# A retention layer and an ELU feed-forward layer on one core: moving weight stores, chunk loads and three VectorE steps to other places of a hand-written order

## The chip, the cores and the metric

The kernel runs on one core of a Trainium2 chip. The metric is the device time of one execution in microseconds (us). A version is timed by the median of several executions; beside them one execution is recorded by the hardware profiler, and all durations below come from that one.

## The reference

Two layers one behind the other, all in float32. The first is a retention layer over B = 4 sequences, H = 8 heads, S = 768 tokens and D = 64 values for each head; the second is a feed-forward layer with ELU on the 4 x 768 = 3072 tokens of 8 x 64 = 512 values.

```python
gamma = 1.0 - 2.0 ** (-5.0 - np.arange(H)); scale = 1.0 / np.sqrt(D)
for t in range(S):
    state = gamma * state + outer(k[t], v[t])      # 64 x 64 for each sequence and head
    y[t] = scale * q[t] @ state
x = y.transpose(0, 2, 1, 3).reshape(3072, 512)
h = x @ w_in                                       # 512 x 2048
g = np.where(h > 0, h, np.exp(np.minimum(h, 0)) - 1)
return g @ w_out                                   # 2048 x 512
```

## The kernel before

**The tiles.** The 3072 tokens are six tiles of 512. A tile is four chunks of 128 tokens; the q, k and v of a chunk are one DMA of 1 MB (`load`, L102, issued at L113) into one of four buffers (`ldpool`), and then one multiplication of v by decay factors on POOL (`scale_v`, L287, operation at L293). Tiles 0 and 1 go through the layers by themselves. Tiles 2 and 3 are the first large block, tiles 4 and 5 the second (`for nb in range(NB)`); the "first large block" of the change is nb = 0.

**Retention** of a tile is cut into five steps (`retention_step`, L1544). Step 0 is the scores of q and k (`scores`, L324: two calls, one for each pair of chunks, in bursts of small matmuls listed as sc L319), step 1 the states (`states`, L373: two calls, matmuls listed as kv L359, then four sums on VectorE for each call; scores and states share four PSUM buffers, two for each call), and steps 2, 3 and 4 are the outputs (matmuls listed as y L415 and y L430), after each of which VectorE makes four products. Steps 2, 3 and 4 write the tile's x, which the first layer reads. The steps are put between the matrix products of another tile, where the order says so. Below, "visit 3" and "visit 4" are steps 3 and 4 of tile 2, which are called from the loop at L1622.

**The feed-forward layer by Strassen's method.** Each product of two matrices is cut into 2 x 2 blocks and made of seven block products; inputs of some of them are differences of blocks (made by VectorE), and their results are added up afterwards. In the second layer this is done twice, one inside the other: seven outer products, each of seven inner products. The inner product i of the outer product k is written (k,i) here. The stages that matter, with their times in the profile:

- 172 to 242 us: the second layer of tile 1 (`second_twice`, L903, matmuls at L924), outer order 1, 2, 6, 7, 5, 3, 4 (`ORDER2`), inner order 1, 2, 6, 7, 5, 3, 4 (`inner`). It is a generator which the loop at L1622 drives; each time it hands back a place ("first", "middle" or the end of an outer product), the loop looks into two dictionaries: VISITS (which visit of tile 2's retention comes here) and LOADS (which of chunks 12 to 15, that is tile 3, is loaded and scaled here). The number counts the outer products from 0, so (1, "first") is the first place inside the second one. `next_input` makes the inputs of later outer products on VectorE meanwhile, and `add` (L936) sums results of inner products.
- 242 to 303 us: the first layer of the first large block. `big_twice` (L1139, matmuls at L1152) makes four of the seven outer products of the first layer, each in two halves: eight halves, at = 0 to 7. A half holds the inner products in the order 1, 2, 6, 7, 5, 4, 3 (matmuls into the PSUM banks pa, pb and pd), and ScalarE copies some of their results (`lift`, L1163). Between them stand retention steps of tile 3, the inputs of the products to come (`xparts`, L1678), and stores of weights (below).
- 303 to 343 us: the other three outer products of the first layer, called M6, M4 and M5 by their numbers (`rest(m, 6)`, `rest(m, 4)`, `rest(m, 5)`; matmuls in `big_rest`, L1199), for eight slices m = 0 to 7 of the hidden values, in the loop over n at L1760. They are added into PSUM on top of a sum that ScalarE copied there (`seed`, L1650; `second_seed`, L1654, copies at L1656). `big_sum` (L1206, operation at L1208) makes the slices of the blocks C21, C12 and C22, `big_elu` (L1210) takes ELU of them (ScalarE at L1214 and L1215, VectorE at L1216), and `big_c11` (L1218, operation at L1220) completes the block C11.
- 343 to 446 us: the second layer of the first large block (`second_big`, L1233, matmuls at L1248, ScalarE's copies of results `ms` at L1256). The inputs of an outer product are four differences, called quarter inputs (`quarters_of`, L892, operations listed at L894); `next(sec)` makes one step of this generator, and its first four steps are the four quarter inputs of the first outer product.
- 446 to 536 us and 538 to 626 us: the same for the second large block, nb = 1.

**What sets the order.** Each engine runs its instructions in the order in which the program issues them; this order is written out by hand. All DMAs go through SP's queue, in program order, and SP holds at a DMA until its buffer is free; what is behind it in the queue is held too.

**Weights.** The combined weights of the second layers lie in DRAM (scratch), and pieces of 256 KB come into a ring of eight buffers `wq` (three more for tile 1). When a product is done with a piece, `done` (L833) hands the buffer back, and `fetch` (L826) issues the next weight DMA at once (L830). For the second large block the weights of its first layer are fetched in the same way, so the first block stores them in DRAM: `send_quarters(j)` (L867: quarters of the outer products j = 1, 2, 3, 7, six DMAs of 128 KB each) and `send_layer(j)` (L880: the planes of M4, M5 and M6, four DMAs of 256 KB each). They only fill a list, and `send_small` (L664) issues what is in it. Before the change a list names one store for each half (`stores`, L1695): none, quarters 2, quarters 3, plane 4, quarters 1, plane 6, quarters 7, plane 5.

**The three VectorE steps.** The last step of `xparts` is M4's input, `sub(t4_, b21, t2)` at L1120: one operation on 128 x 1024 values. In the order before, it comes behind `big_c11(0, 1)` of half 7 (L1732), an add of the same size, and behind `rest(0, 6)` and the second seed (L1755). In the loop over n, the last slice is n = 7 (LAST). At n = 6 two quarter inputs are made, at n = 7 two more ahead of `rest(7, 5)`, and then the sums of tile (slice) 7 into C12 and C22, which ScalarE waits for to take ELU of them. The loads of tile 4's chunks 16 to 19 (`bring`, L1669: load and scaling) stand in halves 4 and 5 and at n = 1 and n = 5.

## Time and the profile before

| what | value |
|---|---|
| median of three runs | 623.34 us (622.74, 623.34, 626.59) |
| the profiled execution: its own time | 628.01 us |
| its span from first to last instruction | 626.2 us |
| mean granted TensorE clock in it | 0.997 |
| instructions | 13424 |
| ScalarE's wait at L1163 for TensorE, over 32 copies | 46.3 us |
| POOL's wait at L293 for chunks, over 16 scalings | 159.8 us |
| bytes moved by DMA, mean rate | 125.14 MB, 200 GB/s |
| weight pieces of 256 KB: DMAs, median from issue to landing | 191, 3.1 us |
| chunks of 1 MB: DMAs, median from issue to landing | 22, 7.7 us |
| stores of 128 KB from `w_all`, and of 256 KB | 24 and 12; 4.1 and 5.2 us |

How to read it: the profile comes from one execution, which took 628.01 us; the span is the stretch in which instructions run. A line of the trace's groups has the engine, the name of the tile written, the line of the kernel, and behind an arrow what the engine waited for. PE is TensorE, DVE VectorE, ACT ScalarE, POOL GpSimd and SP the engine that issues the DMAs. In the list of waits of TensorE the three numbers are the summed wait, how many instructions had it, and the longest one. In a timeline a line has the start, the length and the instruction, and in brackets how long the engine stood idle before it and what ended that. Busy times of TensorE are modelled, so a busy share of 98% does not mean that nothing is left inside a matmul.

### The profile page before, as it was taken

To read this page: it belongs to the slowest core of one execution; us is meant where nothing else is said; L and a number is where in the kernel's file an instruction comes from. 1 tells how busy PE (TensorE), PEld (TensorE's weight loads), DVE (VectorE), ACT (ScalarE), POOL (GpSimd) and SP (SyncE) were. 2 spreads that over 40 slices of the span, in tenths; PEclk is the share of its full clock that TensorE was granted. 3 is DMA by queue.
4 is the path that set the end of the run, shared out by engine and by line. 5 is a ranking of instruction groups with operands and counts; after the bars stand their busy time and mean duration, and the time that the engine had idled before them with its cause. 6 is when DMAs were issued, how large, how long until landed. Compare 5 with 4: busy or idle time off the path is not lost.

```text
span 626.2 us, 13424 instructions
## 1 busy us (share of the span) xinstructions
PE 612.4 (98%) x5446; PEld 481.7 (77%) x5446; DVE 495.3 (79%) x776; ACT 260.9 (42%) x446; POOL 24.9 (4%) x30
## 2 busy tenths in 40 slices
PE   7899999999999999999999999999999999999998
PEld 5774568888888998888444888888888644688886
DVE  5759889989788875777788987898546788888885
ACT  5889744205542111236797310100144789511110
POOL 1012000000000010000110000120000000000000
PEclk8999999999999999999999999999999999999999
DMA  8798568889574997289941445773554422356552
GB/s 298 276 349 324 168 202 267 240 239 273 205 235 124 333 364 268 61 256 277 301 133 68 115 132 156 265 273 108 205 165 144 142 69 86 115 152 185 153 155 113
DMA packets 79278, 125.14 MB, mean 200 GB/s; under 512 B 6128, under 2 KB 46832, under 8 KB 74480
## 3 DMA queue, kind: packets, MB, share of 16 engines
q1 hardware_dynamic: 79216, 124.28, 61.1%
q8 instruction: 43, 0.70, 0.4%
q14 instruction: 19, 0.16, 0.1%
HBM read 94.63 MB, written 29.62 MB: 198 GB/s over the span
## 4 chain that ended last, share of the span: by engine, by line
PE 86%; DMA 6%; DVE 3%; SPq 1%; issue 1%; ACT 1%; DVEq 0%; ACTq 0%
PE pa L1248 15%; PE pa L1152 9%; PE pd L1248 7%; PE pa L1199 6%; PE pd L1152 4%; PE pd L1199 4%; DMA wq<-scratch_dram 4%; PE pb L1248 4%; PE pa L542 3%; PE x L632 3%; PE pa L765 3%; DMA chunk<-in_qkv_dram 2%; PE pb L1152 2%; PE pa L632 2%; PE pb L1199 2%; PE y L415 2%
## 5 line engine op out<-in xcount | busy, mean ns | idle before, releaser
L1256 ACT COPY ms<-pa 128x256 f32<-128x256 f32 x41 | 15.2, 370 | 104.0 <-PE pa L1248 101.0
L1248 PE MATMUL pa<-gC,wq 128*128 128x256 f32 x224 | 53.2, 382 | 0.3 <-ACT ms L1256 0.3
L1248 PEld LDWEIGHTS pa<-gC,wq 128*128 128x128 f32 x224 | 42.0, 190 | 7.5 <-issue 1.0
L1215 ACT ACTIVATE r<-r 128x512 f32<-128x512 f32 x64 | 40.3, 630 | 2.0
L1163 ACT COPY m<-pa 128x512 f32<-128x512 f32 x32 | 18.7, 585 | 46.4 <-PE pa L1152 46.3
L293 POOL TENSOR_TENSOR chunk<-chunk,vf 128x512 f32<-128x512 f32 x16 | 22.2, 1388 | 381.1 <-DMA chunk<-in_qkv_dram 159.8
L1260 DVE TENSOR_TENSOR res<-pd,ms 128x256 f32<-128x256 f32 x26 | 11.0, 422 | 24.2 <-PE pd L1248 14.1
L1152 PE MATMUL pa<-ts,wq 128*128 128x256 f32 x104 | 27.1, 385 | 0.7 <-ACT w_all L1163 0.7
L1248 PE MATMUL pa<-ts,wq 128*128 128x256 f32 x112 | 26.9, 383 | 0.3 <-ACT ms L1256 0.3
L1248 PE MATMUL pd<-w_all,wq 128*128 128x256 f32 x112 | 26.5, 379 | 0.0
L171 ACT ACTIVATE w_all<-wraw 128x1024 uint32<-128x1024 uint32 (+1 forms) x19 | 19.2, 1009 | 15.9 <-DMA wraw<-in_w_dram 5.2
L1248 PE MATMUL pd<-ts,wq 128*128 128x256 f32 x104 | 24.6, 379 | 0.0
L1230 DVE TENSOR_TENSOR gC<-w_all,gC 128x1024 f32<-128x1024 f32 x20 | 24.2, 1261 | 0.0
L1248 PEld LDWEIGHTS pa<-ts,wq 128*128 128x128 f32 x112 | 20.9, 190 | 3.7 <-ACT ms L1256 0.7
L1248 PEld LDWEIGHTS pd<-w_all,wq 128*128 128x128 f32 x112 | 21.3, 190 | 2.9
L1216 DVE SCALAR_TENSOR_TENSOR w_all<-r,w_all 128x512 f32<-128x512 f32 x32 | 21.9, 684 | 1.9 <-ACT r L1215 1.9
L1152 PEld LDWEIGHTS pa<-ts,wq 128*128 128x128 f32 x104 | 19.2, 190 | 5.5 <-ACT w_all L1163 1.1
L1248 PE MATMUL pa<-w_all,wq 128*128 128x256 f32 x96 | 22.9, 381 | 0.0
L173 ACT ACTIVATE w_all<-wraw 128x1024 fp8e4<-128x1024 f32 (+1 forms) x19 | 22.6, 1191 | 0.6
L1214 ACT ACTIVATE r<-w_all 128x512 f32<-128x512 f32 x32 | 20.0, 624 | 6.2 <-DVE w_all L1208 6.2
L1199 PE MATMUL pa<-gC,w_all 128*128 128x512 f32 x48 | 22.1, 592 | 0.0
L1199 PE MATMUL pa<-ts,wq 128*128 128x512 f32 x48 | 22.1, 592 | 0.0
(327 smaller groups left out, 1458.2 us busy)
## 6 DMA issues: line engine op xcount, KB each, us to landing
wq<-scratch_dram SPq DMA_DIRECT2D x191, 256.0 KB, 3.1
chunk<-in_qkv_dram SPq DMA_DIRECT2D x22, 1024.0 KB, 7.7
wraw<-in_w_dram SPq DMA_DIRECT2D x15, 1024.0 KB, 6.1
out_dram<-res SPq DMA_DIRECT2D x7, 512.0 KB, 2.9
scratch_dram<-gT SPq DMA_DIRECT2D x12, 256.0 KB, 4.3
wq<-scratch_dram SPq DMA_DIRECT2D x24, 128.0 KB, 3.0
scratch_dram<-w_all SPq DMA_DIRECT2D x24, 128.0 KB, 4.1
scratch_dram<-w_all SPq DMA_DIRECT2D x12, 256.0 KB, 5.2
```

Source lines behind the costliest of these rows:

```text
L171: nc.scalar.activation(flat, lo, AF.Copy, scale=2.0**-29)
L173: nc.scalar.activation(top, hi.bitcast(FP32), AF.Copy, scale=2.0**-120, saturate=False)
L293: eng.tensor_tensor(out=v, in0=v, in1=vf[:, i].unsqueeze(2).to_broadcast([C, H, D]), op=ALU.mult)
L542: nc.tensor.matmul(hp, lhsT=w[n][:, fi, j // 2, j % 2, :], rhs=xb[:, j, :], start=(j == 0), stop=(j == 3))
L632: nc.tensor.matmul(X[j][:, d, :], lhsT=w[j][:, d * P : d * P + P], rhs=x[j], start=(n == 0 and d == 0), stop=at_end, skip_group_check=True,)
L1152: nc.tensor.matmul(ps[:, f, :], lhsT=w[:, f, :], rhs=big_xs[j][k], start=(begin and f == 0), stop=True, skip_group_check=True,)
L1199: nc.tensor.matmul(ps, lhsT=w[:, k, :], rhs=layer_x[j][:, k], start=False, stop=(k == 1), skip_group_check=True,)
L1214: nc.scalar.activation(r, g, AF.Relu, scale=-1.0)
L1215: nc.scalar.activation(r, r, AF.Exp, scale=-1.0)
L1216: return lambda: nc.vector.scalar_tensor_tensor(g, r, -1.0, g, ALU.add, ALU.max)
L1230: nc.vector.tensor_tensor(out=quarter(to, r, t), in0=quarter(x, r, t), in1=quarter(y, r, t), op=op)
L1248: nc.tensor.matmul(ps, lhsT=w[:, f, :], rhs=ts[j][k][:, f // 2, f % 2, :], start=(begin and f == 0), stop=(f == 3), skip_group_check=True,)
```

## The change

No matrix product, no DMA and no operation of VectorE, ScalarE or POOL is added or taken away. What is moved:

- In tile 1's second layer, visit 3 goes from the end of the first outer product's place to (1, "first"), where visit 4 stood, and visit 4 to (1, "end"). The loads of chunks 14 and 15 go from (4, "middle") and (5, "first") to (5, "end") and (6, "middle"); those of 12 and 13 stay at their places, so that chunk 12's now stands ahead of visit 4 in the program.
- In the first half of the first large block, states(3, 0) stands in the middle, and scores(3, 1) and states(3, 1) at the end. Before, scores(3, 1) stood in the middle and both states at the end.
- The stores: planes 4 and 6 at half 0, quarters 2 and plane 5 at half 1, quarters 3 at half 2, quarters 1 at half 5 and quarters 7 at half 7. The number of DMAs and of bytes is the same.
- Chunks 16 to 19 are loaded and scaled at n = 0, 1, 3 and 5 of the loop over n, and no longer in halves 4 and 5.
- In both large blocks M4's input takes the place of `big_c11(0, 1)` at half 7, and that add goes behind `rest(0, 6)`, ahead of the second seed.
- In both large blocks the two quarter inputs at n = 6 go away from there: two of the four are made at n = 7 ahead of `rest(7, 5)`, and two behind the loop. So tile 7's sums into C12 and C22 stand ahead of the last two quarter inputs.

```diff
--- before.py
+++ after.py
@@ -1617,8 +1617,8 @@
         pass
     flush()
     retention_step(2, 2)
-    step, VISITS = 0, {(0, "end"): 3, (1, "first"): 4}
-    LOADS = {(1, "first"): 0, (2, "end"): 1, (4, "middle"): 2, (5, "first"): 3}
+    step, VISITS = 0, {(1, "first"): 3, (1, "end"): 4}
+    LOADS = {(1, "first"): 0, (2, "end"): 1, (5, "end"): 2, (6, "middle"): 3}
     for s in sec:
         if s == "first":
             step += 1
@@ -1692,11 +1692,11 @@
             if at in parts_of:
                 some(xparts, parts_of[at][place])
 
-        stores = [
-            lambda: None, lambda: send_quarters(2), lambda: send_quarters(3), lambda: send_layer(4, range(NQ)),
-            lambda: send_quarters(1), lambda: send_layer(6, range(NQ)), lambda: send_quarters(7),
-            lambda: send_layer(5, range(NQ)),
-        ]
+        stores = {
+            0: lambda: (send_layer(4, range(NQ)), send_layer(6, range(NQ))),
+            1: lambda: (send_quarters(2), send_layer(5, range(NQ))), 2: lambda: send_quarters(3),
+            5: lambda: send_quarters(1), 7: lambda: send_quarters(7),
+        }
         for at, (j, sub) in enumerate(ORDER1):
             if at == 4:
                 held_x = [ldpool.tile([P, 2048], FP32, name="chunk", tag="chunk") for _ in range(2)]
@@ -1720,7 +1720,7 @@
                 end("C11", 1)
             if nb == 0:
                 if at == 0:
-                    scores(3, 1)
+                    states(3, 0)
                 elif at == 1:
                     retention_step(3, 3)
             run(tail)
@@ -1728,31 +1728,32 @@
                 seed(0)
             next(cur)
             tail = cur
-            if at in (5, 7):
-                big_c11(0, at // 7)
+            if at == 5:
+                big_c11(0, 0)
+            if at == 7:
+                some(xparts, 1)
             if at == 6:
                 end("C11", 0)
             if at in (6, 7):
                 begin("C11", {6: 1, 7: 5}[at])
             if nb == 0:
                 if at == 0:
-                    retention_step(3, 1)
+                    scores(3, 1)
+                    states(3, 1)
                 elif at == 1:
                     retention_step(3, 4)
                     run(tail)
             side(at, 2)
-            if nb == 0:
-                if at in (4, 5):
-                    bring(groups[0], at - 4)
+            if nb == 0 and at in stores:
                 stores[at]()
                 send_small()
         sec = second_big(nb, (lambda: run(big_x(2))) if more else lambda: None)
         LAST = 2 * NQ - 1
         next(tail)
         rest(0, 6)
+        big_c11(0, 1)
         second_seed(0)
         end("C11", 4)
-        some(xparts, 1)
         run(tail)
         seed(1)
         begin("C11", 2)
@@ -1795,17 +1796,16 @@
                 end("C11", 3)
             if n in (0, 2):
                 begin("C11", 6 + n // 2)
-            if more and n in (1, 5):
-                bring(groups[0], 2 + n // 4)
+            if more and n in (0, 1, 3, 5):
+                bring(groups[0], (n + 1) // 2)
             if n == LAST:
                 next(sec)
                 next(sec)
             rest(n, 5)
             sum_("C12", n)
             sum_("C22", n)
-            if n == LAST - 1:
-                next(sec)
-                next(sec)
+        next(sec)
+        next(sec)
         next(sec)
         begin("C12", LAST)
         next(sec)
```

## The prediction

> **What bounds the kernel now.** I read the page's busy shares first, then its chain that ended last, then the waits of TensorE, then the timelines of TensorE, VectorE and SyncE around each wait. The shares and the chain:
>
> ```profile
> PE 612.4 (98%) x5446; PEld 481.7 (77%) x5446; DVE 495.3 (79%) x776; ACT 260.9 (42%) x446; POOL 24.9 (4%) x30
> ...
> PE 86%; DMA 6%; DVE 3%; SPq 1%; issue 1%; ACT 1%; DVEq 0%; ACTq 0%
> ```
>
> TensorE is busy for 612.4 of 626.2 us, and the change takes no matmul away. So an edit can gain only what TensorE waits. The list of TensorE's waits gives the places:
>
> ```profile
> PE pd L924 <- DMA wq<-scratch_dram: 1.3, 2, 0.9
> PE pd L1199 <- DVE ts L1120: 1.0, 1, 1.0
> PE pd L1199 <- ACT w_all L1163: 0.9, 1, 0.9
> ...
> PE y L430 <- issue: 0.8, 1, 0.8
> PE pa L1152 <- ACT w_all L1163: 0.7, 1, 0.7
> ...
> PE pa L1248 <- ACT ms L1256: 0.6, 2, 0.3
> ```
>
> These six lines (5.3 us) are all that the change can reach; the other waits lie before 172 us or where nothing moves. The chain in order of time shows that from 217 to 241 us the transfers set the pace:
>
> ```profile
> 217.40 8.62 DMA wq<-scratch_dram
> 226.04 7.42 DMA chunk<-in_qkv_dram
> 233.52 7.65 DMA wq<-scratch_dram
> ```
>
> **The change part by part.** (k,i) is inner product i of outer product k of tile 1's second layer; its 8 matmuls take 0.895 us (start to start in TensorE's timeline).
>
> *Visits 3 and 4 of tile 2 later.* No instruction is added. In the trace visit 3 runs from 195.24 to 197.95, with 0.83 us of "issue" in it, and visit 4 begins at 201.72. After the change (2,1), (2,2), (1,3), (1,4) begin at 195.24 and end at 198.8, visit 3 (2.71 - 0.83 = 1.88) ends at 200.7, (2,6), (2,7), (2,5) end at 203.4, and visit 4 follows. VectorE's four products of visit 4 (2.48 us at 202.48) move behind the fourth next_input step and the inputs of (6,.), which so come earlier; nothing reads tile 2's x before 236.42, so they cost nothing. The "issue" wait stands where 2 visits with one product between them follow each other. Visit 4, which has four products (3.6 us) ahead of it, shows none. After the change each visit has at least three ahead. Bounds 0 to -0.8; nearest row visit 4, so **-0.8**.
>
> The Trainium skill (Runtime: NRT & Kernel Launch, "Instruction fetch mechanics") says that instructions arrive in blocks of 256 while earlier ones run, and that crossing a block is mostly hidden. By that rule the burst of short instructions would not be what makes this wait, and spreading the bursts would gain 0 here and not 0.8. No row here shows which it is.
>
> *Load 12 stands ahead of visit 4 now.* It takes a buffer whose last reader is visit 4, so SP holds at it and the weight fetches behind it wait. In the trace it is issued 0.75 us after visit 4 begins (202.47), so now at 203.4 + 0.75 = 204.1, 1.7 later. The four fetches ahead of it go 2.7 earlier, since their products do; the three behind it (204.00 to 205.8) go at 204.5 to 205.2. So the transfers of this stretch change places and little time is lost. The next wait on weights, at 224.71 (0.2 now), has bounds -0.2 and +1.7; I take **+0.3**, near the lower end: the DMA share is only 0.67 in 202 to 204, so the time that SP holds is partly idle today.
>
> *Loads 14 and 15 later.* This is where a stall goes:
>
> ```profile
> 226.04 0.33 SPq L113 DMA_DIRECT2D chunk<-in_qkv_dram  x1
> ...
> 230.81 0.48 SPq L113 DMA_DIRECT2D chunk<-in_qkv_dram  x1
> ...
> 234.25 1.13 PE L924 MATMUL pd<-ts,wq 128*128 128x128 f32 x8 [0.34 <-DMA wq<-scratch_dram]
> ...
> 241.30 1.13 PE L924 MATMUL pd<-ts,wq 128*128 128x128 f32 x8 [0.94 <-DMA wq<-scratch_dram]
> ```
>
> The two loads stand ahead of the last weights of tile 1. At 385 GB/s (window 224 to 226) 1 MB takes 2.7 us and 256 KB 0.68. The weight of (4,4), issued at 233.52, landed 7.65 later at 241.17, and its product starts at 241.30. Behind the change no 1 MB load stands before it: both waits go, **-1.3** (bounds 0 and -1.5, with the 0.2 at 224.71). What is late next is load 15. From the transfer that landed at 230.67 go 8.5 weights and stores (5.8), load 14 (2.7), 3.4 us of weights and stores, load 15 (2.7): it lands at 245.3. POOL's scaling (1.04) ends at 246.3. TensorE reaches scores(3,1), now where the states stood (248.05), at 248.05 - 1.3 - 0.8 + 0.3 = 246.2, and states(3,1) 1.1 later. So 0.9 us of cover; if it is gone, the delay is paid in full. The other order in the first half, states(3,0), scores(3,1), states(3,1), costs nothing: the same matmuls in two bursts; states(3,1) takes the PSUM buffers of states(3,0), whose sums (4 x 0.42) are through 1.9 us after its matmuls, and there is a product and the scores between (2.2).
>
> *Stores early, loads 16 to 19 late.* In the trace load 16 and six quarter stores stand ahead of three weight pieces:
>
> ```profile
> 285.99 0.38 SPq L113 DMA_DIRECT2D chunk<-in_qkv_dram  x1
> 286.43 5.87 SPq L664 DMA_DIRECT2D scratch_dram<-w_all  x6
> 292.40 3.42 SPq L830 DMA_DIRECT2D wq<-scratch_dram  x3
> ...
> 297.83 1.10 PE L1152 MATMUL pa<-ts,wq 128*128 128x256 f32 x4 [0.68 <-ACT w_all L1163]
> ```
>
> The line names ScalarE's copy, but the same product in the second block starts at 492.82, before that copy (493.02); the piece issued at 292.40 landed 5.3 later, at 297.7. So it is a late weight, and without the load and the stores ahead of it it goes: **-0.7** (bounds 0 and -0.7). The 18 stores now sent in halves 0 and 1 fall into 248 to 262, where the DMA share is 0.22 to 0.03 until 256. Only one fetch stands behind the first eight: 255.58, held there by TensorE anyway; eight stores need some 8 x 0.5 us of SP from 248.5. Quarter stores of outer product 1 go at half 5, some 12 us ahead of the first C21 sum (305.32) that overwrites them. Loads 16 to 19 have their first readers at 352.25 (sc L319) and land some 9 us behind their issue at the slowest (load 16, 8.95), so m = 0 (303) to m = 5 (332) is early enough. SP waits 18.4 us at load 19 today with no fetch behind it until 344.8, and still does. POOL's four scalings now lie in 303 to 338, one more than today; a contended one costs VectorE 0.25 to 0.86 us (L1216 at 0.93 for 0.68, L936 at 1.55 for 0.69), hidden by VectorE's 6.7 us of idle time in 303 to 348; without that cover up to 0.9.
>
> *M4's input ahead of C11's add.* Both are 1.22 us of VectorE and change places.
>
> ```profile
> 301.96 1.22 DVE L1120 TENSOR_TENSOR ts<-xt,gC 128x1024 f32<-128x1024 f32 x1
> ...
> 303.33 1.96 PE L1199 MATMUL pd<-ts,w_all 128*128 128x512 f32 x4 [0.96 <-DVE ts L1120]
> ```
>
> The input ends at 303.18 and the product starts 0.15 later. In the second block it ends at 498.11 and the product starts 0.10 later, so there too it is the input, though the list names ScalarE. In the add's place it starts at 299.63 and ends at 300.85. What is late next is the copy into the accumulator (L1656, ends 302.12), as TensorE comes free at 302.2. So 0.96 and 0.92 go: **-1.9** (bounds -0.5, if ScalarE's copy that ends at 302.99 and 497.90 were needed, and -2.1). The add ends at 302.6, ahead of its reader at 303.55.
>
> *Tile 7's sums ahead of two quarter inputs.* VectorE is full from 339.66 to 349. The present wait (0.28) comes from ScalarE, which waits 2.32 us for tile 7's C21 sum; with the sum at 342.35 instead of 344.46 that goes. But the third input comes behind tile 7's two sums: from 339.66 stand eight steps of 0.6, two inputs of 1.17 and 0.3 of waits for ScalarE ahead of it (7.4), so it ends at 348.3 instead of 346.88, and inner product 7 wants it at 348.07: 0.3 us of new wait. In both blocks **0** (bounds -0.6 and +0.9).
>
> Sum: -0.8 + 0.3 - 1.3 - 0.7 - 1.9 + 0 = -4.4 us. The profiled execution took 628.01 us (span 626.2 and 1.8 around it), so 623.6 for its like; that is 4.67 above the median of 623.34, and I put the whole shift on the median: **618.9**.
>
> **The rivals.** (B) The waits on transfers move and do not go: load 12's hold gives back what loads 14 and 15 free, and an early store delays another weight. Then only M4's 1.9 and part of the rest stay: 623.34 - 2.3 = 621.0. For it: DMA is at 0.9 to 1.08 of its share from 204 to 242. Against it: the loads moved stand behind the last urgent weight. (C) Slower: load 15 comes late and scores(3,1) waits. If SP reaches it only at 243.6, where it sends its last store of the stage, and it takes the 9.7 us that it took today, it lands at 253.3: 7.1 of wait at 246.2, 618.9 + 7.1 = 626.0. It decides from a landing at 250.6 on. Against it: the queue has little behind it then. (D) The "issue" wait is not tied to the burst and stays in visit 3: 618.9 + 0.8 = 619.7. For it: visit 2 (192.59), a burst of the same kind, shows none. Against it: the wait stands in the second of two bursts with one product between. By the rule of the page named above, this is the case.
>
> **How the numbers follow.** All bounds at their best give -0.8 - 0.2 - 1.5 - 0.7 - 2.1 - 0.6 = -5.9 (617.4), all at their worst 0 + 1.7 + 0 + 0 - 0.5 + 0.9 = +2.1 (625.4). Forecast 0.48 (own range 617.4 to 620.3, the latter with the wait at 224.71 and M4 half way to their worse ends), D 0.14, B 0.23, C 0.10, more gained than worked out 0.05. The range 617.2 to 623.0 leaves out that last case and the larger part of C. A measurement of this kernel tells about 1% (6.2 us) from no change. Faster by over 1% (below 617.1) is only the last case: 0.05. Slower by over 1% (above 629.6) needs C with a landing 3.6 us later still: 0.03 of its 0.10. Within 1%: 0.92.
>
> **What would show it.** Right: no wait on wq at L924 after 230 us, none at L1152 near 296, TensorE at L1199 (pd) starting with no wait on L1120, in both blocks; y L430 without "issue". Wrong: a wait of sc L319 or kv L359 on the chunk near 246; a wait at 224 grown beyond 1 us; a new wait of pd L1248 on L894 over 0.5 us; or the sums in place and the time not moved, which would say that the profiled execution's waits are longer than those of the timed ones.

## The result and the profile after

The changed kernel takes 622.49 us (median of 20 runs, 620.40 to 626.01), the kernel before 624.34 us (20 runs, 622.74 to 628.44). By these medians the gain is 1.9 us. The ratio is 0.9959 with an interval of 0.9944 to 0.9975, which is a gain of 2.6 us (1.6 to 3.5); a second comparison, below, gave 0.9966 (0.9947 to 0.9985), 2.1 us. The forecast was a gain of 4.4 us. The time lies in the range and within 1% of before, but the gain is only 0.4 to 0.6 of the forecast.

The busy shares, one DMA queue (packets, MB, share of the DMA engines; needed further down) and the chain of the changed kernel, from its page:

```profile
PE 611.4 (98%) x5446; PEld 480.9 (77%) x5446; DVE 496.7 (80%) x776; ACT 261.0 (42%) x446; POOL 21.2 (3%) x30
...
q8 instruction: 43, 0.70, 0.4%
...
PE 86%; DVE 4%; DMA 3%; ACT 3%; issue 2%; SPq 0%; DVEq 0%
```

TensorE's work is the same. In the chain the transfers fall from 6% to 3%, and "issue" rises from 1% to 2%. The list of TensorE's waits (engine, line, what it waited for; sum, times, longest) says where:

```profile
PE pa L924 <- DMA wq<-scratch_dram: 1.3, 1, 1.3
PE y L415 <- issue: 0.8, 2, 0.5
PE sc L319 <- issue: 0.6, 1, 0.6
...
PE pd L1248 <- DVE ts L894: 0.2, 1, 0.2
```

Of the six lines that the prediction showed, all are gone in the form that they had: no wait on L1120 and none at L1152, no "issue" at y L430, none on ms. Three new ones stand in their place. (Of the two waits at y L415 the longer one, 0.53, is at 25.39 us, ahead of all that was moved; the other, 0.27, is new.) TensorE's timeline has their times:

```profile
221.02 1.13 PE L924 MATMUL pa<-ts,wq 128*128 128x128 f32 x8 [1.25 <-DMA wq<-scratch_dram]
...
246.79 0.35 PE L319 MATMUL sc<-chunk 64*64 64x64 f32 x9 [0.62 <-issue]
...
251.26 0.50 PE L415 MATMUL y<-chunk 64*64 64x64 f32 x18 [0.27 <-issue]
```

The first lies in the stretch in which load 12 was moved ahead of visit 4 in SP's queue. It is also a sign that the prediction named for being wrong, a wait on weights near 224 us grown beyond 1 us: 221.02 is 221.94 on the time base of the profile before. The other two lie in the first half of the first large block and just behind it, where the prediction put a cost of nothing.

Two executions can be laid beside each other by TensorE's instructions, since they are the same ones but for their order. I cut the trace at fixed matmuls and took the time from start to start. Up to the first product of tile 1's second layer (184.89 us in the first profile of before) the kernels have the same instructions, and yet that part took 182.2 to 184.9 us in the executions below: this is noise of the beginning, and I leave it out. From there on (us, worked out from the start times in the traces; the first two columns are two executions of the kernel before, the next two of the changed kernel):

| stretch | before | before again | changed | changed again |
|---|---|---|---|---|
| A: visits 3 and 4 (first to 131st matmul of L924) | 24.50 | 24.19 | 23.35 | 23.35 |
| B: load 12's weights (to the 249th) | 13.18 | 13.18 | 14.67 | 14.57 |
| C: last weights of tile 1 (to the first L1152) | 19.70 | 17.99 | 17.36 | 17.36 |
| D: first half of the first large block | 11.29 | 11.29 | 12.81 | 13.11 |
| E: last two halves, to the first L1199 | 12.22 | 12.13 | 11.30 | 11.30 |
| F: M4's first products, both blocks | 9.23 | 9.23 | 7.01 | 7.00 |
| G: first products of the second layer, both blocks | 14.90 | 14.89 | 14.64 | 14.64 |
| from A to the end | 441.35 | 439.24 | 437.44 | 437.64 |

All other stretches agree within 0.05 us. The means, 440.3 and 437.5, differ by 2.8 us, close to the 2.6 and 2.1 of the two comparisons. So these stretches hold the answer: A, C, E, F and G gained, B and D gave back some 3 us.

### The profile page after: what moved, and what is told of

It reads as the page before. It is cut to its first block, busy times and chain, and to the rows that moved or that the text cites. A ratio compares the mean times of both kernels' runs of the same rounds, so it can differ in the third digit from the quotient of the medians.

```text
span 621.4 us, 13415 instructions
## 1 busy us (share of the span) xinstructions
PE 611.4 (98%) x5446; PEld 480.9 (77%) x5446; DVE 496.7 (80%) x776; ACT 261.0 (42%) x446; POOL 21.2 (3%) x30
## 4 chain that ended last, share of the span: by engine, by line
PE 86%; DVE 4%; DMA 3%; ACT 3%; issue 2%; SPq 0%; DVEq 0%
PE pa L1248 15%; PE pa L1152 9%; PE pd L1248 8%; PE pa L1199 6%; PE pd L1152 4%; PE pa L765 4%; PE pd L1199 4%; PE pb L1248 4%; PE x L632 3%; DMA wq<-scratch_dram 2%; PE pa L924 2%; PE pa L542 2%; PE pb L1152 2%; PE pa L632 2%; PE pb L1199 2%; PE y L415 2%
## 5 line engine op out<-in xcount | busy, mean ns | idle before, releaser
L1163 ACT COPY m<-pa 128x512 f32<-128x512 f32 x32 | 18.7, 585 | 48.9 <-PE pa L1152 48.8
L293 POOL TENSOR_TENSOR chunk<-chunk,vf 128x512 f32<-128x512 f32 x16 | 18.0, 1124 | 381.3 <-DMA chunk<-in_qkv_dram 201.1
L1152 PE MATMUL pa<-ts,wq 128*128 128x256 f32 x104 | 26.9, 384 | 0.0
L1152 PEld LDWEIGHTS pa<-ts,wq 128*128 128x128 f32 x104 | 19.3, 190 | 4.5 <-ACT m L1163 0.8
L1248 PEld LDWEIGHTS pd<-ts,wq 128*128 128x128 f32 x104 | 19.7, 190 | 3.2 <-DVE ts L894 0.6
L1199 PE MATMUL pa<-ts,wq 128*128 128x512 f32 x48 | 22.1, 592 | 0.0
L1199 PE MATMUL pa<-gC,w_all 128*128 128x512 f32 x48 | 22.1, 592 | 0.0
```

The source lines that it names most:

```text
L293: eng.tensor_tensor(out=v, in0=v, in1=vf[:, i].unsqueeze(2).to_broadcast([C, H, D]), op=ALU.mult)
L1152: nc.tensor.matmul(ps[:, f, :], lhsT=w[:, f, :], rhs=big_xs[j][k], start=(begin and f == 0), stop=True, skip_group_check=True,)
L1163: nc.scalar.copy(o, ps)
L1199: nc.tensor.matmul(ps, lhsT=w[:, k, :], rhs=layer_x[j][:, k], start=False, stop=(k == 1), skip_group_check=True,)
L1248: nc.tensor.matmul(ps, lhsT=w[:, f, :], rhs=ts[j][k][:, f // 2, f % 2, :], start=(begin and f == 0), stop=(f == 3), skip_group_check=True,)
```

## The experiments

Each run is compared with the kernel before on the same chip. Letters are the stretches above.

**M4's input alone.** The add and the input change places, nothing else.

```diff
-            if at in (5, 7):
-                big_c11(0, at // 7)
+            if at == 5:
+                big_c11(0, 0)
+            if at == 7:
+                some(xparts, 1)
...
         rest(0, 6)
+        big_c11(0, 1)
         second_seed(0)
         end("C11", 4)
-        some(xparts, 1)
```

> The kernel before with one part of the change alone: M4's input ahead of C11's add in both large blocks. Theory (the prediction's step holds): the waits of TensorE at L1199 on L1120 near 303 us and on the second block near 498 us (0.96 and 0.92) are both gone, nothing comes in their place, 1.9 us faster than before, ratio 0.9970. Rival 1 (ScalarE's copies, ending 302.99 and 497.90, hold the product too): the two waits shrink to about 0.65 each and the gain is 0.5 us, ratio 0.9992. Rival 2 (the add, now behind, makes a later reader wait): a new wait at L1210 to L1216 or in M4's products of slice 1, and a gain under 1 us.

Ratio 0.9955 (0.9934 to 0.9976), medians 623.13 and 625.29. Both waits are gone, F is 7.01 us, 2.22 shorter, and nothing comes in their place: the step holds. The gain is larger than the listed idle time of 1.88: where nothing waits, a matmul starts before the record of the one ahead has ended (0.22 us apart at 0.38 long in the products just ahead of these), and behind a wait it does not. So 0.96 us of wait cost 1.13 from start to start, 0.92 cost 1.09.

**The edits around tile 1 alone.** The visits, loads 14 and 15, and the new order in the first half.

```diff
-    step, VISITS = 0, {(0, "end"): 3, (1, "first"): 4}
-    LOADS = {(1, "first"): 0, (2, "end"): 1, (4, "middle"): 2, (5, "first"): 3}
+    step, VISITS = 0, {(1, "first"): 3, (1, "end"): 4}
+    LOADS = {(1, "first"): 0, (2, "end"): 1, (5, "end"): 2, (6, "middle"): 3}
...
                 if at == 0:
-                    scores(3, 1)
+                    states(3, 0)
...
                 if at == 0:
-                    retention_step(3, 1)
+                    scores(3, 1)
+                    states(3, 1)
```

> The kernel before with the edits around tile 1's second layer alone: visits 3 and 4 one place later, loads 14 and 15 later, states(3,0) in the middle of the first half and scores(3,1) with states(3,1) at its end. The stores stay where they were. By the prediction's terms: -0.8 (issue) +0.3 (load 12) -1.3 (loads 14, 15) = -1.8 us, ratio 0.9971. Theory now: load 12's hold costs 1.0 to 1.4 us in one wait on wq at L924 near 221 us, and the wait for the instruction stream comes back in the half's bursts: sc L319 waits about 0.6 near 246 us, since a boundary of 256 TensorE instructions falls into that burst; net -0.3 to -0.8, ratio 0.9987 to 0.9995. Rival (the new waits for the instruction stream come from the early stores' traffic): with the stores at their old places neither sc L319 nor y L415 waits, net -1.2 us or better, ratio 0.998 or lower.

Ratio 0.9992 (0.9975 to 1.001), where the prediction's terms gave 0.9971. A lost 1.15 us against the first profile of before, B grew by 1.29, C fell by 2.34 and D grew by 0.99. In this execution E, which this part does not touch, was 0.7 longer than in the first profile. So this part of the change, which was to bring 1.8 us, brings next to nothing by the time. The wait at sc L319 is there with the stores at their old places; the one at y L415 in stretch D is not.

**The stores back in their old halves.**

```diff
-        stores = {
-            0: lambda: (send_layer(4, range(NQ)), send_layer(6, range(NQ))),
...
+        stores = [
+            lambda: None, lambda: send_quarters(2), lambda: send_quarters(3), lambda: send_layer(4, range(NQ)),
...
-            if nb == 0 and at in stores:
+            if nb == 0:
```

> The changed kernel with the weight stores back in the halves where they stood before (loads 16 to 19 stay late). Theory (boundary of 256 instructions in a burst, and the block's packet late because the DMA queues are full): the packet behind the y L415 wait starts about 1 us after the boundary before it and no longer 2.3, so the wait at y L415 near 251 us (0.27) goes; the one at sc L319 near 246 us (0.62) stays, because the stores reach the queue only at 245.6, behind its packet at 244.3. Gain against the changed kernel 0.3 to 0.6 us, if the wait on a weight near 296 us (0.68 before) does not come back; with it the time is that of the changed kernel. Rival A (traffic plays no part, only where the boundary falls): both waits stay with their sizes, time as the changed kernel, ratio to before 0.996. Rival B (stores alone make both): both go, 0.9 us and more gained, ratio 0.9945.

Ratio 0.9929 (0.9903 to 0.9955). D is 11.73 us, 1.1 shorter than in the changed kernel: the wait at y L415 is gone and that at sc L319 is down to a gap of 0.29. The late weight near 296 us does not come back, since load 16 is still late. More was gained than the gap of 0.49 at y L415, so the size of the sc L319 wait is not fixed. The interval just overlaps that of the changed kernel (0.9944 to 0.9955).

**Load 12 behind visit 4.** One word in the changed kernel; the visit stands ahead of the load at the same place of the loop.

```diff
-    LOADS = {(1, "first"): 0, (2, "end"): 1, (5, "end"): 2, (6, "middle"): 3}
+    LOADS = {(1, "end"): 0, (2, "end"): 1, (5, "end"): 2, (6, "middle"): 3}
```

> The changed kernel with load 12 behind visit 4 (at the end of the second outer product and not at its first place), so that SP does not hold at it with weight fetches behind. Theory (the hold of 4.7 us at load 12, 198.4 to 203.1, starves the weight stream): the fetches behind it go out at their own time, the wait on wq at L924 near 221 us (1.25) falls below 0.3, 1.0 us or more gained against the changed kernel, ratio to before 0.9943 or lower. Rival (the stretch is bound by the bytes moved, the order does not matter): the load still stands ahead of the same bytes and the wait stays at 1 us or more, or moves to another product of the stretch; ratio 0.996 as the changed kernel.

Ratio 0.9933 (0.9906 to 0.9960); the interval overlaps that of the changed kernel, but in the trace no wait on wq at L924 is left in the list. SP's timeline shows why, in the changed kernel first (start, length, what SP issues):

```profile
196.21 2.11 SPq L830 DMA_DIRECT2D wq<-scratch_dram  x3
203.09 0.33 SPq L113 DMA_DIRECT2D chunk<-in_qkv_dram  x1
203.47 4.14 SPq L830 DMA_DIRECT2D wq<-scratch_dram  x7
```

and with load 12 behind visit 4:

```profile
196.01 5.64 SPq L830 DMA_DIRECT2D wq<-scratch_dram  x5
201.99 0.33 SPq L113 DMA_DIRECT2D chunk<-in_qkv_dram  x1
203.52 2.11 SPq L830 DMA_DIRECT2D wq<-scratch_dram  x3
```

The load leaves at the same moment of the program in both (visit 4 sets it), but in the changed kernel SP stands at it for 4.7 us (198.36 to 203.09), with three weight fetches queued behind it. SP's list of waits has this hold:

```profile
SPq L113 <- PE y L430: 5.2, 2, 4.9
```

In the kernel before the same line reads 0.8 in all. While SP stands, the transfers run out. The view of stretches has the busy time of PE, PEld, DVE, ACT and POOL, and at the end of each line the granted clock, the DMA share and the GB/s; the first line is of the kernel before, the other two of the changed kernel:

```profile
202.00:204.00 2.00, 2.00 (x71) 1.93 (x63) 1.64 (x4) 0.00 (x0) 0.00 (x0) 1.00 0.67 189
...
200.00:202.00 2.00, 2.00 (x20) 2.00 (x19) 1.79 (x3) 0.27 (x1) 0.00 (x0) 1.00 0.43 156
202.00:204.00 2.00, 2.00 (x73) 1.81 (x72) 1.26 (x3) 0.27 (x1) 0.00 (x0) 1.00 0.00 0
```

Over the whole hold the share is 0.40; with load 12 behind visit 4 the same stretch of the program (197.3 to 202.0 us there) has 0.63. What was held is missing later: stretch B is 13.52 us here and 14.67 in the changed kernel. D was 11.46 in this run, almost as before.

**The kernel before and the changed kernel once more.** No edit.

> The kernel before once more, unchanged, as a second profiled execution of it. Theory (the first profile of before had waits on transfers that other executions have not, or have shorter): the ratio is 1.000 within its interval, and of the waits at L924 on wq (0.34 near 234, 0.94 near 241), L1152 (0.68 near 298) and y L430 on issue (0.83 near 198) at least one is gone or differs by over 0.2 us, while the waits at L1199 on L1120 (0.96) and L1248 on ms (0.28) come back within 0.03. Rival (every wait belongs to the program): all of them come back within 0.1 us.

Ratio 1.0011 (0.9992 to 1.003). TensorE's waits in this second execution of before:

```profile
PE pd L1199 <- DVE ts L1120: 1.0, 1, 1.0
PE pd L1199 <- ACT w_all L1163: 0.9, 1, 0.9
...
PE pa L1152 <- DMA wq<-scratch_dram: 0.6, 1, 0.6
PE pa L1248 <- ACT ms L1256: 0.5, 2, 0.3
PE y L430 <- issue: 0.5, 1, 0.5
PE pd L924 <- DMA wq<-scratch_dram: 0.4, 1, 0.4
```

The waits on engines (L1120, L1163 in the second block, ms) come back to the hundredth. The waits on transfers do not: 0.4 where the first profile had 0.34, 0.94 and 0.2, and 0.5 of "issue" for 0.83. The wait at L1152 is named by its DMA now, as the prediction argued.

> The changed kernel once more, unchanged. Theory: ratio 0.994 to 0.998; the wait on wq at L924 near 221 (1.25) comes back at 0.8 to 1.4, since the hold of SP at load 12 makes it in the first look and in both runs that kept it; the waits for the instruction stream at sc L319 and y L415 come back at the same instructions (behind the 55th and the 46th matmul of their bursts) if at all, with sizes from 0 to 0.7 that go with how late the block's packet starts. Rival (the waits for the instruction stream are fixed by the program): 0.62 and 0.27 again.

Ratio 0.9966 (0.9947 to 0.9985). The wait near 221 is back (1.15). The issue waits stand behind the same matmuls, the 55th and the 46th, with other sizes, 0.37 and 0.81:

```profile
245.58 0.35 PE L319 MATMUL sc<-chunk 64*64 64x64 f32 x9 [0.37 <-issue]
250.59 0.50 PE L415 MATMUL y<-chunk 64*64 64x64 f32 x18 [0.81 <-issue]
```

**The stores and loads 16 to 19 alone.** The new `stores` and the `bring` lines of the change, in the kernel before.

```diff
-                if at in (4, 5):
-                    bring(groups[0], at - 4)
...
-            if more and n in (1, 5):
-                bring(groups[0], 2 + n // 4)
+            if more and n in (0, 1, 3, 5):
+                bring(groups[0], (n + 1) // 2)
```

> The kernel before with one part of the change alone: the weight stores early and the loads of chunks 16 to 19 late. By the prediction's term: the wait at L1152 near 297.8 us (0.68) goes, -0.7 us, ratio 0.9989. Theory now: a wait there costs its idle time and some 0.24 more (start to start 0.92 in the first profile), but it is 1.37, 0.68 and 0 in the three profiles that had the stores and load 16 at the old places, so on the mean some 0.9 us go; the first two halves have more traffic, and no wait for the instruction stream comes in them since the bursts stand as before: ratio 0.998 to 0.999. Rival (the stores in halves 0 and 1 delay the instruction blocks there by themselves): a new issue wait of 0.3 or more at kv L359 near 249 or y L415 near 252.7, and no gain.

Ratio 0.9993 (0.9974 to 1.0011): a gain of 0.4 us, a little less than expected, and not to be told from none. E is 11.30, and D is 11.29, exactly that of before: the early stores alone cost the first halves nothing.

**The instruction stream shifted.** If an issue wait stands where TensorE runs into the next block of its instructions, its place in the stream must be fixed by counting. In the trace, each 64x64 matmul is two instructions (weight load and matmul). The edit adds 16 calls, and the trace then has 32 more matmuls (5478 in place of 5446): each call makes two. So the stream is shifted by 64 instructions, and not by the 32 of the expectation; the waits were to move 32 matmuls forward and not 16.

```diff
     unread(1, TB)
-    for n in range(25):
+    for n in range(41):
```

> The changed kernel with 16 more of the unread 64x64 matmuls with which TensorE begins (41 in place of 25 at L1391; their results are never read). Each is two instructions (weight load, matmul), so every instruction behind stands 32 later in TensorE's stream. Theory (the waits named issue stand where TensorE's stream passes a multiple of 256 instructions, counted in the trace from one fixed offset): what wait there is moves 16 matmuls forward in its burst, from behind the 55th to behind the 39th of sc L319 near 246 us, and from behind the 46th to behind the 30th of y L415 near 251 us. The time changes by less than 0.5 us from the changed kernel. Rival (the wait belongs to that matmul, by its operands or by what VectorE does): it stays behind the 55th and the 46th.

Ratio 0.9983 (0.9965 to 1.0001). That is some 1 us slower than the changed kernel's 0.9966 of the same comparison, where less than 0.5 was expected; the intervals overlap, and the trace has new waits near the start. I numbered the weight loads, matmuls and semaphore instructions in TensorE's records. Every wait over 0.15 us that the profile names "issue", in all runs, stands at a number that is 193 more than a multiple of 256. Some of them (worked out from the traces):

```
before   4289 = 16*256 + 193   y L430   (visit 3)
changed   961 =  3*256 + 193   y L415   (tile 0)
changed  5569 = 21*256 + 193   sc L319
changed  5825 = 22*256 + 193   y L415
shifted   449 =  1*256 + 193   sc L319
shifted   705 =  2*256 + 193   pa L518
shifted   961 =  3*256 + 193   kv L359  (tile 0; y L415 without the shift)
```

The two waits in D could not be seen to move, since both are gone (D is 11.35): the boundary ahead of them moved from behind the burst scores(3,0) into it, and the block between now takes 8.2 us. Near the start three waits stand at the new boundaries (the last three lines), and the changed kernel has no wait at those matmuls. The wait belongs to the boundary, not to the matmul.

**Visits 3 and 4 back at their old places.**

```diff
-    step, VISITS = 0, {(1, "first"): 3, (1, "end"): 4}
+    step, VISITS = 0, {(0, "end"): 3, (1, "first"): 4}
```

> The changed kernel with visits 3 and 4 back at their places of before (so load 12 stands behind visit 4 again). Theory (load 12's hold behind the later visit 4 is the cause of the wait near 221 us, and the backlog that it leaves makes the instruction packets of the first half late): the wait on wq at L924 near 221 is gone (1.4 us start to start), the issue wait of visit 3 at y L430 is back (0.5 to 0.8), and the two issue waits in the first halves (1.5 to 1.8 together, start to start) shrink below 0.6. Net 1.5 to 2.2 us faster than the changed kernel, ratio 0.9925 to 0.994. Rival (the order of the first half alone makes its two waits): they stay at 1.5 us; net 0.5 us faster than the changed kernel, ratio 0.9955.

Ratio 0.9953 (0.9931 to 0.9975). My theory fell here in its second half: the issue wait of visit 3 is back (0.63) and the wait near 221 is down to 0.38 (B is 14.00), but the two waits of D stay (0.62 and 0.27, D 12.81). So load 12's hold is not what makes the waits in D.

**The new order of the first half alone.**

```diff
                 if at == 0:
-                    scores(3, 1)
+                    states(3, 0)
...
                 if at == 0:
-                    retention_step(3, 1)
+                    scores(3, 1)
+                    states(3, 1)
```

> The kernel before with one part of the change alone: states(3,0) in the middle of the first half, scores(3,1) and states(3,1) at its end; loads, stores and visits as before. Theory (an issue wait needs both a boundary of 256 instructions that is reached some 3.9 us or less behind the one before it and a packet that starts late behind a full queue): the packets start about 1 us behind the boundary as in the kernel before, and the halves lose 0 to 0.3 us; ratio 0.9995 to 1.0005. Rival (the order of the bursts alone costs it): the first half is 1 us or more longer, with issue waits behind the 55th matmul of sc L319; ratio 1.002.

Ratio 1.0004 (0.9983 to 1.0025), D 11.40: no issue wait in D. The order alone costs 0.1 us.

**Load 12 behind visit 4 again, and with the old stores.** The second kernel has the edits of "load 12 behind visit 4" and of "the stores back in their old halves" together.

> The changed kernel with load 12 behind visit 4, once more and unchanged from the first such run. Theory: no wait on wq at L924 over 0.3 us, the first half within 0.4 us of its length in the kernel before, ratio 0.9915 to 0.995, so 1.2 to 2.8 us faster than the changed kernel (0.9959 and 0.9966 in its two comparisons). Rival (the first such run was a lucky one): the wait near 221 or the issue waits are back, ratio 0.996.

> The changed kernel with load 12 behind visit 4 and with the stores in the halves of before (loads 16 to 19 late as in the change). Theory: both sources of the lost time are away, the two halves within 0.2 us of the kernel before; what can come back is the late weight near 296 us, which did not with the old stores once load 16 was late. Ratio 0.992 to 0.9945, the same as with load 12 alone within the interval. Rival (the old stores bring the late weight back): a wait at L1152 of 0.5 or more, ratio 0.9955.

Load 12 again: 0.9936 (0.9914 to 0.9958). No wait near 221 (B 13.36), but D is 13.63, with issue waits of 1.17 and 0.54, so the short D of the first such run was chance and the gain in B was not. Over all traces B is 14.47 to 15.06 in the five with load 12 ahead of visit 4, and 13.18 to 14.04 in the thirteen with it behind. With the old stores too: 620.27 us, ratio 0.9923 (0.9894 to 0.9951), B 13.18, D 11.73, no wait at L1152. This is the lowest ratio of all versions. By the ratios it is 2.2 to 2.7 us below the changed kernel, though the intervals overlap a little (0.9944 to 0.9951).

**New order with late loads, new order with early stores.** What was open: which traffic makes the instruction block late. Both have the edits of "the new order of the first half alone", on the kernel before, and one more: the first the late loads 14 and 15 (below), the second the early stores (the edit of "the stores and loads 16 to 19 alone").

```diff
-    LOADS = {(1, "first"): 0, (2, "end"): 1, (4, "middle"): 2, (5, "first"): 3}
+    LOADS = {(1, "first"): 0, (2, "end"): 1, (5, "end"): 2, (6, "middle"): 3}
```

> The kernel before with two parts of the change: the new order of the first half, and loads 14 and 15 later; the stores and the visits as before. Theory (the late loads are in the queues when the first half's instruction block is asked for): the packet behind the sc L319 boundary starts 1.5 us or more behind the boundary before it and the wait there is 0.3 or more start to start; the y L415 boundary has its packet at 0.8 to 1.4 us and no wait. Rival (the early stores are needed for it): no wait at either, as with the new order alone (0.11 in that run).

> The same kernel as the run with the new order and the late loads, a second execution. Theory: a wait of 0.3 us or more at sc L319 again, none at y L415. Rival: none at either.

> The kernel before with two parts of the change: the new order of the first half, and the early stores (with loads 16 to 19 late); loads 14 and 15 and the visits as before. Theory (the late loads make the first wait, and only a stop at the first boundary pushes the second block's request among the stores): neither sc L319 nor y L415 waits, the first half is within 0.3 us of its length in the kernel before. Rival (the early stores delay the second packet by themselves): its packet starts 2 us or more behind the boundary, and y L415 waits 0.3 or more.

> The same kernel as the run with the new order and the early stores, a second execution. Theory: no wait at either boundary. Rival: y L415 waits 0.3 or more.

With the early stores D is 11.38 and 11.40, no issue wait in either. With the late loads it is 11.44 in one execution and 13.09 in the other, whose TensorE timeline reads:

```profile
245.04 1.04 PE L319 MATMUL sc<-chunk 64*64 64x64 f32 x55
247.50 0.35 PE L319 MATMUL sc<-chunk 64*64 64x64 f32 x9 [1.43 <-issue]
...
250.78 1.16 PE L415 MATMUL y<-chunk 64*64 64x64 f32 x64
```

These four runs are single executions, of which only the traces are read. A wait was expected in both executions with the late loads and came in one; the DMA records explain both. The queue "q8 instruction" has 43 packets and 0.70 MB (the page above): 16 KB each, and TensorE's 11,100 records are 43.4 times 256. So I take a packet for TensorE's next block. For the block that begins at 5569 (sc L319; in the old order kv L359) and the one at 5825 (y L415), the table has how long behind the boundary ahead of it the packet starts, and the gap at the boundary, from the start of the last instruction ahead of it to that of the first behind it (us, worked out from the traces):

| run | order, loads 14/15, stores | packet for sc L319, gap | packet for y L415, gap |
|---|---|---|---|
| before (two), M4 alone, stores alone | old, early, old or early | -1.5 to -0.7, 0 | 0.8 to 1.0, 0 |
| new order alone | new, early, old | 0.18, 0 | 0.87, 0 |
| new order, early stores (two) | new, early, early | 0.44 and 0.29, 0 | 0.99 and 0.96, 0 |
| new order, late loads (two) | new, late, old | 1.48, 0; 3.18, 1.64 | 1.33 and 1.34, 0 |
| edits around tile 1; changed with old stores | new, late, old | 2.27, 0.84; 1.85, 0.29 | 1.32 and 1.32, 0 |
| visits back at their old places | new, late, early | 2.39, 0.83 | 2.30, 0.48 |
| changed, changed again | new, late, early | 2.31, 0.84; 2.05, 0.59 | 2.27, 0.49; 2.60, 1.03 |
| load 12 moved (two) | new, late, early | 1.54, 0; 2.85, 1.38 | 1.34, 0; 2.54, 0.76 |
| load 12 moved, old stores | new, late, old | 1.81, 0.29 | 1.34, 0 |

In every case with a gap TensorE goes on 2.2 to 2.5 us after the packet's start. The block ahead of the sc L319 boundary takes 3.93 us of its own with the new order (3.92 with the old one). So the gap is packet delay + 2.4 - 3.93: 3.18 gives 1.65 (1.64 seen), 2.31 gives 0.8 (0.84), 1.48 gives 0. With the new order and loads 14 and 15 early the packet starts 0.2 to 0.4 us behind the boundary, with them late 1.5 to 3.2. The data traffic goes with it: in the 2 us behind that boundary the transfers move 40 to 72 GB/s in all runs with early loads, where load 15 has landed 4.3 to 5.1 us ahead of the boundary, and 281 to 377 GB/s with late loads, where it lands 1.3 to 2.8 us behind it (worked out from the traces). So with the new order the late loads make the first wait. In the shifted run the packet is as late (3.2), but the block ahead takes 8.2 us, and there is no gap. What the order does to this packet is smaller: with early loads it starts 0.7 to 1.5 us ahead of the boundary in the old order. No run has the old order with late loads, so it stays open whether they would make a wait there too. The early stores do nothing by themselves; the y L415 block is late only where the stores are early and TensorE has stopped at sc L319. That the stop pushes the second request in among the stores fits all of these rows, but no run shows the request itself.

## Why the prediction was right or wrong

The steps, with what they measured. The measured size is from start to start: for A, C and E the mean over all executions with the old places against those with the new ones, since these waits vary; for the others the kernel before against the two executions of the changed kernel.

| step | predicted | measured |
|---|---|---|
| visits 3 and 4 (A) | -0.8 | -1.0 |
| load 12 (B) | +0.3 | +1.4 |
| loads 14 and 15 (C) | -1.3 | -1.0 |
| order of the first half (D) | 0 | +1.7 (1.5 and 1.8) |
| stores early, loads 16 to 19 late (E) | -0.7 | -0.6 |
| M4's input (F) | -1.9 | -2.2 |
| tile 7's sums (G) | 0 | -0.3 |
| sum | -4.4 | -2.0 (by the time: -2.6 and -2.1) |

**Load 12 was mis-sized.** "So the transfers of this stretch change places and little time is lost" is the sentence that failed, and "near the lower end" the choice. The issue time was right (worked out as 204.1 on the old time base, measured 203.09 plus the 0.92 by which this profile was ahead, 204.0). But the DMA share of 0.67 in 202 to 204, which I took for idle time to spare, fell to nothing in the changed kernel while SP held, and a stream that then runs at a share of 1.04 (210 to 226 us) and 0.99 (226 to 242 us) has no room to make up what SP did not issue in 4.7 us. The cost of 1.4 is near the upper bound of 1.7.

**"The other order in the first half ... costs nothing: the same matmuls in two bursts" failed.** I counted engines and buffers, and not TensorE's instruction stream, although the same view had just given the wait in visit 3. In the first half 256 instructions run in 3.9 us, and the late loads, another part of the same change, made the packet of the next 256 late. The order alone costs 0.1 us; with the late loads D is 11.4 to 13.6 over ten executions, 0.2 to 2.3 more than before, and 1.5 and 1.8 more in the two of the changed kernel. I put this under the order, where the prediction had nothing; since the late loads were never run with the old order, it could stand under them as well. The sum had no term for what the two do together.

**The visits were right, for a reason that was only half right.** The wait of visit 3 went (A fell by 1.0, and with the visits put back the wait returned). I tied it to two bursts with one product between them. What the runs show is a boundary of 256 instructions in the burst, reached 3.0 us behind the one before, and a packet that started 1.9 us behind it. The changed kernel reaches that boundary 6.1 us behind, so it has no wait there; this is the spreading that the step spoke of. The Trainium skill (Runtime: NRT & Kernel Launch, "Instruction fetch mechanics") has blocks of 16 KiB and 256 instructions, and the packets and the count agree; that crossing a block is mostly hidden holds for most boundaries here, and not for these (0.3 to 1.6 us).

**M4's input, the late weight, loads 14 and 15, load 15's cover.** M4's input held in both blocks. The other two gains held only as means. With loads 14 and 15 at their old places C is 17.37 to 19.70 over seven executions, with the late places 17.4 in all, so the gain is 0 to 2.3. With the old places of the stores and of load 16 E is 11.30 to 12.91, with the new ones 11.30, so the gain is 0 to 1.6. Load 15 was to land at 245.3 and landed at 243.94 (244.9 on the old time base); scores(3,1) began at 245.14 and did not wait for it, so rival C did not come. Tile 7's sums gained 0.3: the wait on ms went, and the new wait on the third quarter input (L894) came, with 0.2 in one block and not 0.3 in both. It was not run by itself.

**The rivals.** B described what happened around tile 1: load 12's hold gave back what loads 14 and 15 freed (1.4 against 1.0). Its price, a gain of 2.3, came out right, but by chance: in B's own sum little more than M4 stays, and here A, C and E paid too and the first half gave back the rest. D had the issue wait staying; it left its place and came back in two others.

**The shift onto the median.** I put waits from one execution of before on all of them. That execution took 628.01 us, and its waits on transfers in C and E were longer than those of the next one by 1.8 us; the waits on engines were the same in both. A second error worked against it: a wait costs some 0.2 us more than its listed idle time. Priced from start to start, the first profile gives -1.15, -2.34 and -0.92 for A, C and E (-4.4 in all); the listed idle times gave -2.8; the mean over the executions is -2.6. So these two errors cancelled, by luck, and what is left of the difference, some 2.4 us (-4.4 against -2.0), is B (1.1) and D (1.7) less the 0.6 by which F and G did better, and 0.2 by which A, C and E fell short. The forecast of 618.9 also started from 623.34, the median of three runs; the twenty give 624.34, so 1.0 of the 3.6 us between 618.9 and 622.49 lies there.

## What to carry to other kernels

A load that waits for its buffer is priced by what is queued behind it on the issuing engine: put it behind the last reader in the program, even if it leaves at the same moment. Bursts of short matmuls are to be counted in instructions as well as in time: where 256 of them run in under 4 us while large transfers are in flight, TensorE can stand still, and moving a burst or a load by one place makes or takes away such a wait. Waits on engines came back within a few hundredths in a second profile; waits on transfers need a second profile of the same kernel before a gain is promised from them.

## What the runs showed of the hardware

- TensorE's instructions come in DMA packets of 16 KB (43 on q8), one for 256 instructions, and where TensorE waits at a boundary of the table it goes on 2.2 to 2.5 us after the start of the packet's transfer. The packets have a queue of their own, but their start goes with the data in flight: in the first half with the new order it was 0.2 to 0.4 us behind the boundary before it at 40 to 72 GB/s, and 1.5 to 3.2 us at 281 to 377 GB/s.
- A wait on TensorE costs 0.16 to 0.21 us more than the idle time that the profile lists. Against the usual distance of 0.11 between two starts at L924, the start behind the wait at 241.30 (0.94 listed) was 1.10 later, and the one at 221.02 (1.25 listed) 1.42; at sc L319 0.62 listed cost 0.83. Where nothing waits, the records overlap: 8 matmuls of L924 span 1.13 us from first start to last end, and 0.895 from start to start of two products.
